# Loading one batch's v straight into rows, spreading another's in four 32-row tiles, and moving a mixer step between two transposes

## The chip, the cores and the metric

The kernel runs on one core of one Trainium2 chip. The metric is the device time of one execution in microseconds (us).

PE is the TensorE matmul stream, PEld its weight loads, DVE the vector engine, ACT the scalar engine, POOL GpSimd, SP the sync engine. "L640" is a line of the kernel's source. The same line has other numbers in the changed kernel: the mixer's hidden matmuls are L630 before and L629 after, the output matmuls L640 and L639, the spreading of v L561 and L560. In experiments that put removed code back they are L633, L643 and L564.

## The reference

Eight batches, eight heads, 576 rows, head size 64. Attention with a causal mask and a bias from a cumulative sum of s; its output is the input of a low-rank token mixer and a two-layer channel mixer.

```python
scores = q @ k.T / sqrt(64)
cum    = cumsum(max(s, 0))
scores = where(causal, -1e9, scores + min(-(cum_i - cum_j), 0))
attn   = softmax(scores);  x = attn @ v              # 8 x 576 x (8*64)
u      = x + (x.T @ U @ V).T                         # rank 32
out    = u + relu(u @ w_ch1) @ w_ch2                 # 512 -> 2048 -> 512
```

## The kernel before

Heads are worked in pairs, four pairs a batch: pair n = 4 is the first pair of batch 1. For each pair the program emits `transposes(n)` (q and k turned on PE, copied out of PSUM into a slot by ACT or DVE), `scores(n)` (matmuls, exponentials on ACT) and `values(n)` (the product with v). These are interleaved by hand with the channel mixer of an earlier batch, `chanmix`, that comes in pieces of four 512-column matmuls: `step_fill` and `fill_with` take the next pieces.

For `values`, v must lie with one row per partition (`v_slots`). Batches 2 to 7 are loaded straight into that layout, with 256-byte runs. Batches 0 and 1 were loaded raw, four rows to a partition in 1 KB runs, and PE spread them with selection matmuls:

```python
def v_tiles(b, js, copies):
    vt = v_slots[b % 3]
    if b == 0:
        pvs = [pwork() for _ in js]                  # one PSUM bank each, of four
    else:
        both = pscore()
        pvs = [both[:, ds(i * 512, 512)] for i in range(len(js))]
    for t in range(4):
        for j, pv in zip(js, pvs):
            pick, src = sel[ds(32 * j, 32), ...], v_raw[ds(32 * j, 32)]   # 32 rows of PE
            nc.tensor.matmul(pv, lhsT=pick, rhs=src[:, :, t, :], start=(t == 0), stop=...)
    for j, pv, copy in zip(js, pvs, copies):
        copy(vt[:n_rows, j, :, 0:D], pv)             # PSUM -> SBUF, DVE (batch 0), ACT (batch 1)
# ...
v_tiles(0, (0, 1), (dve, dve)); step(S2); step(S2)   # batch 0, in two pairs and a rest
v_tiles(0, (2, 3), (dve, dve)); step(S2, S2)
# ...
weave("S5 S5 T6 S5 T6 S5 S6 R0 T7 S6 R1 T7 S6 R2 S6")   # R0 to R2 spread batch 1
```

Two more pieces matter. `copies(n, hh, par)` decides which engine copies the transposes of head hh out of PSUM; for n = 4 it was ACT for head 0 and DVE for head 1. In the main loop, the token mixer of the batch before (`seqmix`) has a first step whose small result, uxT, DVE must copy before PE can go on:

```python
if n > 2 * PB and n + 1 < NP:
    run(transposes(n + 1))      # four DVE copies of the slot
step(mixing)                    # 20 small matmuls, then uxT on DVE
```

In the first 20 us PE also runs `spin` in places: matmuls on a constant whose result nobody uses, to keep PE busy over waits.

The softmax here doesn't subtract the row's maximum and nothing guards it: scores larger than these inputs give would overflow.

## Time and profile before

Time: 381.25 us median of 3 runs (381.01 to 381.28). The profile is of a further execution at full clock, which took 381.74 us, half a microsecond more than the median.

| | before |
|---|---|
| PE busy | 371.0 us of a 380.0 us span |
| matmuls | 3583 |
| ACT busy, 42 to 46 us | 4.00 of 4.00 us |
| idle PE named by its list of waits | 5.8 us, of which 1.3 before the first matmul; nearly all before 120 us |

From the page (part 1: busy time, share of the span, instructions):

```profile
PE 371.0 (98%) x3583; PEld 210.5 (55%) x3583; DVE 217.3 (57%) x453; ACT 199.8 (53%) x300; POOL 65.0 (17%) x103
```

PE's busy time says which engine to look at, not how well it does. The Trainium skill, "Trainium Kernel Development and Optimization", Performance Expectations, calls matmul busy time a bad metric, because matmuls are pipelined. So I read what PE waited for. From the list of PE's waits (us in total, times, longest; its first line, the 1.3 us before the first matmul, and the waits under 0.4 us are left out):

```profile
PE pscore L375 <- DMA slot<-hT: 1.2, 1, 1.2
PE pwork L477 <- DVE uxT L473: 0.9, 1, 0.9
PE pwork L630 <- ACT slot L310: 0.6, 1, 0.6
PE pscore L561 <- ACT v_slot L570: 0.4, 1, 0.4
```

In order: the first scores waited for the rows of s; the token mixer for uxT; a hidden matmul for a PSUM bank that ACT was still copying out; the spreading of batch 1 for ACT's copies.

The timeline of PE has start, duration, line, operands, count, and in brackets the idle time before. A group's own duration contains the pipeline's tail, so the cost of a group is the start of the next minus its own. Batch 1's spreading, and its surroundings:

```profile
50.94 0.61 PE L375 MATMUL pscore<-slot 68*128 68x128 bf16 x6
51.48 1.04 PE L561 MATMUL pscore<-hT,sel 32*128 32x512 bf16 x8
52.45 1.04 PE L640 MATMUL pwork<-w_sb,hT 128*128 128x512 bf16 x4
...
56.50 0.60 PE L375 MATMUL pscore<-slot 68*128 68x320 bf16 x4
57.47 0.59 PE L561 MATMUL pscore<-hT,sel 32*128 32x512 bf16 x2 [0.37 <-ACT v_slot L570]
57.99 1.04 PE L640 MATMUL pwork<-w_sb,hT 128*128 128x512 bf16 x4
```

Eight matmuls in two row tiles take 52.45 - 51.48 = 0.97 us; four rounds of a 512-column matmul (0.216 us each in this trace) would be 0.86. The group left out, at 54.12 us, takes 0.97 as well.

### The profile page before, as it was taken

The numbers are of one execution on the slowest core, as the hardware profiler recorded it, in microseconds if no ns is written. First come the engines' busy times: TensorE is split into PE (matmuls) and PEld (weight loads), VectorE is DVE, ScalarE is ACT, GpSimd is POOL, SyncE is SP. The second block draws the span as 40 slices with busy tenths as digits, with TensorE's granted clock in tenths as the row PEclk, the third lists the DMA queues.
The fourth block names the chain that finished last, engine by engine and source line by source line (L and its number), as shares of the span: only waits on it lengthen the run. The fifth ranks groups of instructions, "written<-read, shape, count | busy, mean of one in ns | idle before, by whom it ended". The sixth has DMA issues, their size and how long they took to land.

```text
span 380.0 us, 8508 instructions
## 1 busy us (share of the span) xinstructions
PE 371.0 (98%) x3583; PEld 210.5 (55%) x3583; DVE 217.3 (57%) x453; ACT 199.8 (53%) x300; POOL 65.0 (17%) x103
## 2 busy tenths in 40 slices
PE   8899999999999999999999999999999999999996
PEld 3575556766655666565655665666555544444443
DVE  8785356877777766876678666876753232002012
ACT  3876996657741676147724773457561530620620
POOL 8985316006001400140014000000000000000000
PEclk9999999999999999999999999999999999999999
DMA  7999999949946991599159924220313031301002
GB/s 107 174 209 205 200 160 117 151 113 121 117 41 113 161 124 21 124 160 123 23 91 169 139 32 75 75 73 19 74 47 100 19 72 68 83 28 73 11 29 83
DMA packets 86110, 37.29 MB, mean 98 GB/s; under 512 B 66424, under 2 KB 80472, under 8 KB 86072
## 3 DMA queue, kind: packets, MB, share of 16 engines
q0 software_dynamic: 47216, 18.44, 49.3%
q1 hardware_dynamic: 38856, 18.31, 25.8%
q8 instruction: 28, 0.46, 0.5%
q14 instruction: 10, 0.08, 0.1%
HBM read 37.25 MB, written 9.70 MB: 124 GB/s over the span
## 4 chain that ended last, share of the span: by engine, by line
PE 88%; ACT 6%; DVE 3%; DMA 2%; issue 1%; SPq 0%; ACTq 0%; DVEq 0%
PE pwork L640 31%; PE pwork L630 30%; PE pscore L375 10%; PE pwork L435 8%; PE pwork L293 3%; ACT pT L390 1%; ACT slot L310 1%; ACT hT L662 1%; DMA slot<-hT 1%; PE pwork L677 1%; PE pscore L630 1%; PE pwork L464 1%; DVE uT L489 1%; DVE slot L310 1%; DMA hT<-in_s_dram 1%
## 5 line engine op out<-in xcount | busy, mean ns | idle before, releaser
L630 PE MATMUL pwork<-uT,w_sb 128*128 128x512 bf16 x560 | 135.1, 379 | 1.0 <-ACT slot L310 0.6
L640 PE MATMUL pwork<-w_sb,hT 128*128 128x512 bf16 x560 | 135.3, 379 | 0.2 <-ACT hT L662 0.2
L662 ACT ACTIVATE hT<-pwork 128x512 bf16<-128x512 f32 x140 | 84.4, 608 | 86.9 <-PE pwork L630 86.6
L310 DVE COPY slot<-pwork 64x576 bf16<-64x576 bf16 x111 | 88.8, 800 | 12.3 <-PE pwork L293 10.0
L390 ACT ACTIVATE pT<-pscore 128x1024 bf16<-128x1024 f32 x57 | 57.4, 1025 | 59.8 <-PE pscore L375 59.8
L630 PEld LDWEIGHTS <-w_sb 128*128 128x128 bf16 x576 | 51.0, 98 | 51.7 <-issue 2.3
L640 PEld LDWEIGHTS <-hT 128*128 128x128 bf16 x560 | 49.0, 98 | 50.2 <-issue 2.9
L700 DVE TENSOR_TENSOR o_sb<-pwork,u_sd 128x512 f32<-128x512 f32 x31 | 21.4, 691 | 65.1 <-PE pwork L640 64.4
L375 PE MATMUL pscore<-slot 68*128 68x128 bf16 (+1 forms) x506 | 54.9, 246 | 1.3 <-DMA slot<-hT 1.2
L375 PEld LDWEIGHTS <-slot 68*128 68x128 bf16 x570 | 41.8, 97 | 23.9 <-issue 1.5
L320 DVE TENSOR_TENSOR pT<-pT,keep 128x512 bf16<-128x512 bf16 (+1 forms) x81 | 28.6, 353 | 38.4 <-ACT pT L407 23.2
L435 PEld LDWEIGHTS <-pT 128*128 128x128 bf16 x870 | 32.4, 97 | 10.1 <-issue 0.3
L435 PE MATMUL pwork<-v_slot,pT 128*128 128x65 bf16 x870 | 34.5, 194 | 0.0
L445 DVE TENSOR_TENSOR x_sb<-pwork,rec 128x320 bf16<-128x320 f32 x64 | 31.4, 491 | 2.1
L401 ACT ACTIVATE pT<-pscore 128x1024 bf16<-128x1024 f32 x29 | 30.2, 1040 | 2.9 <-PE pwork L375 1.5
L108 POOL DMA_DIRECT2D q_sd<-in_q_dram x12 | 9.4, 782 | 122.1 <-PE pwork L293 114.5
L225 POOL DMA_DIRECT2D v_slot<-in_v_dram x24 | 21.3, 902 | 10.5 <-DMA w_sb<-in_moe_w_ch_dram 8.2
L444 DVE RECIPROCAL rec<-pwork 128x5 f32<-128x5 f32 x64 | 12.2, 191 | 16.3 <-PE pwork L435 15.7
L293 PEld LDWEIGHTS <-q_sd 72*128 72x128 bf16 x256 | 14.7, 98 | 10.0 <-DMA q_sd<-in_q_dram 0.9
L293 PE MATMUL pwork<-identity,q_sd 72*128 72x72 bf16 x256 | 18.0, 196 | 0.0
L293 PE MATMUL pwork<-identity,k_sd 72*128 72x72 bf16 x256 | 17.9, 198 | 0.1
L310 ACT COPY slot<-pwork 64x576 bf16<-64x576 bf16 x17 | 13.5, 797 | 1.4 <-PE pwork L293 1.2
(110 smaller groups left out, 202.5 us busy)
## 6 DMA issues: line engine op xcount, KB each, us to landing
out_dram<-o_sb SPq DMA_DIRECT2D x35, 256.0 KB
w_sb<-in_moe_w_ch_dram POOLq DMA_DIRECT2D x4, 1024.0 KB, 12.0
q_sd<-in_q_dram POOLq DMA_DIRECT2D x6, 576.0 KB, 8.7
k_sd<-in_k_dram POOLq DMA_DIRECT2D x6, 576.0 KB, 13.8
v_slot<-in_v_dram POOLq DMA_DIRECT2D x24, 128.0 KB, 15.6
hT<-in_v_dram POOLq DMA_DIRECT2D x2, 512.0 KB, 13.6
q_sd<-in_q_dram POOLq DMA_DIRECT2D x4, 144.0 KB, 5.0
k_sd<-in_k_dram POOLq DMA_DIRECT2D x4, 144.0 KB, 5.8
```

What stands on the lines that cost most here:

```text
L293: nc.tensor.transpose(tps[hh][:, c, t2, :], src[:, 2 * hp + hh, ds(t2 * 128, 128)], identity[:TP, :TP],)
L310: copies(n, hh, par)(dst[:, :, :, :, par], tp[par * D : par * D + D].rearrange("p c t m -> p c m t"),)
L320: nc.vector.tensor_tensor(dst, dst, keep[:, :, 0:w].to_broadcast([128, n_tiles, w]), op=ALU.min)
L375: nc.tensor.matmul(dst, lhsT=slot[0:KA, hh, ds(S + j * 128, 128)], rhs=slot[0:KA, hh, lo:hi], start=True, stop=True,)
L390: nc.scalar.activation(pT[:, hh, 0:1024], near, EXP, scale=scale)
L401: nc.scalar.activation(pT[:, :, 1024:1536], mid.rearrange("p (a b) -> p a b", a=2), EXP, scale=scale)
L435: nc.tensor.matmul(po[:, i, :], lhsT=pT[:, hh, ds(place(j, i), 128)], rhs=vt[:, j, h, :], start=(j == 0), stop=(j == i), skip_group_check= ...
L445: nc.vector.tensor_tensor(x_sb[:, hp, :, ds(hh * D, D)], po[:, :, 0:D], rec.to_broadcast([128, 5, D]), op=ALU.mult,)
L630: nc.tensor.matmul(f1, lhsT=w1_sb[:, kt, ds(nf * 128, 128)], rhs=u[:, kt, :], start=(kt == 0), stop=(kt == 3),)
L640: nc.tensor.matmul(f2, lhsT=hT[:, nf, ds(i * 128, 128)], rhs=w2_sb[:, nf, :], start=(nf == 0), stop=(nf == NF - 1 and not more), skip_grou ...
L662: nc.scalar.activation(hT[:, nf, :], f1, RELU)
L700: nc.vector.tensor_tensor(o_sb.rearrange("p (a b) -> p a b", a=4), f2.rearrange("p (a b) -> p a b", a=4), u_sd[:, :, i, :], op=ALU.add,)
```

## The change

The intent: take PE work and PE idle time out of the first 120 us.

1. v of batch 1 is loaded like that of batches 2 to 7; its 18 spreading matmuls and five ACT copies go, and one piece of the channel mixer is put in at two places (word "F").
2. v of batch 0 is spread in four 32-row tiles at once. The group stands behind two steps of scores (six matmuls each) and two `spin` matmuls.
3. The rows of s for head 1 of pair 0 are sent before those of head 0.
4. For pair 4, DVE copies head 0 and ACT head 1.
5. The token mixer's first step stands between the two heads' transposes; the order at the very end is changed a little.

```diff
-        for hh in range(2):
+        for hh in (1, 0) if n == 0 else (0, 1):
             nc.sync.dma_start(out=slots[n][D:KA, hh, 0 : 2 * S], ...)
...
-        on_act = hh == 0 and (n in (0, 1, 4, 5, 7, 8, 9, 10) or n == 2 and par == 0)
+        on_act = hh == (n == 4) and (n in (0, 1, 4, 5, 7, 8, 9, 10) or n == 2 and par == 0)
...
-        if b == 0:
-            pvs = [pwork() for _ in js]
-        else:
-            both = pscore()
-            pvs = [both[:, ds(i * 512, 512)] for i in range(len(js))]
+        pvs = [pwork() for _ in js]
+        if len(js) == 4:
+            spin(2, pvs[0])
+            yield
...
-    v_tiles(0, (0, 1), (dve, dve))
     step(S2)
+    vs = v_tiles(0, (0, 1, 2, 3), (dve, dve, dve, dve))
+    step(vs)
     step(S2)
-    v_tiles(0, (2, 3), (dve, dve))
+    drain(vs)
     step(S2, S2)
...
-    load_v_raw(1)
-    init_v(nc.gpsimd, v_slots[1])
+    load_v(1)
...
-    weave("S5 S5 T6 S5 T6 S5 S6 R0 T7 S6 R1 T7 S6 R2 S6")
-    weave("V4 V4 S7 V5 S7 V5 S7 T8 S7 T8 V6 V6 S8 V7 S8 V7 T9 S8 T9")
-    weave("S8 S9 M1 S9 M1 M1 S9 M1 S9 M1 M1")
+    weave("S5 S5 T6 S5 T6 S5 S6 T7 S6 T7 S6 F S6")
+    weave("V4 F V4 S7 V5 S7 V5 S7 T8 S7 F T8 V6 V6 S8 V7 S8 V7 T9 S8 T9")
+    weave("S8 S9 M1 S9 M1 S9 M1 M1 S9 M1 M1")
...
         if b == B:
             fill_with(3)
-            step(mixing)
-            fill_with(2)
-            step(mixing)
-            fill_with(2)
+            for _ in range(3):
+                step(mixing)
+                fill_with(2)
         if n > 2 * PB and n + 1 < NP:
-            run(transposes(n + 1))
-        step(mixing)
+            for at, _ in enumerate(transposes(n + 1)):
+                step_fill()
+                if at == 0:
+                    step(mixing)
```

More of the change, by code (lines that the diff above doesn't have):

```diff
@@ L794 @@
     nc.gpsimd.memset(pT_early[1][:, :, 1600:], 1.0)
-    v_tiles(0, (4,), (dve,))
+    drain(v_tiles(0, (4,), (dve,)))
     step(S3)
@@ L847, in weave @@
         for word in order.split():
+            if word == "F":
+                fill_with(1)
+                continue
             kind, n = word[0], int(word[1:])
@@ L853, in weave @@
                     made[word] = scores(n, pT_of(n))
-                elif kind == "R":
-                    v_tiles(1, ((0, 1), (2, 3), (4,))[n], (act, act))
-                    made[word] = iter(())
                 elif kind == "V":
```

## The prediction

> **What bounds it now.** TensorE: by the page 371.0 us busy of a 380.0 us span, and 88% of the chain of waits. The stretches view shows full granted clock, and almost no idle PE from 130 us to the last matmul. So only PE work or PE idle time removed counts. The list of PE's waits holds about 5 us, nearly all before 120 us: first rows of s (slot from hT) 1.17 us at 12.96; bank held by ACT's slot copy 0.64 us at 37.00; v copies on ACT 0.37 us at 57.47; uxT copy on DVE 0.90 us at 113.00.
>
> **Terms of the change, in us of PE's chain (timeline of PE).**
>
> 1. Batch 1's spreading matmuls (18 of 32 rows x 512) go away. In the timeline they cost with their lead-in 1.07 (at 51.4), 1.07 (at 54.0), and at 57.5 0.52 plus 0.53 idle. Sum 3.2. Five ACT copies of 0.59 go too. The added fill steps only move work. Saving 3.2.
>
> 2. Batch 0's spreading: 16 matmuls in two pairs cost 2 x 0.97. As four tiles at once I estimate one group of 0.97, from the seqmix step, whose four 32-row x 512 matmuls take 0.33 us together although one alone takes 0.216. The Trainium skill, "TensorEngine Tiling (Array Packing)", Key Properties, says that tiles run in parallel and that changing the mode drains the engine; this trace agrees (0.33 for four, about 0.10 lead at a switch). Two spins give back 0.43. But all four banks become ready together and later than the first pair does now, and DVE then needs 5 copies of 0.65 to 0.68 in a row; tile 4's copy would end near 23.1 us instead of 22.8, and values(0) waits for it. Together with term 3, I credit only 0.3 at the end of values(0).
>
> 3. Rows of head 1 issued first: the issues on SP are 0.57 us apart, so head 1's scores and the ACT chain start that much earlier. Mostly absorbed by term 2's copies.
>
> 4. Pair 4's copies swapped between ACT and DVE: ACT comes to its copies only at 35.35, after two ReLUs; DVE should free the first bank about 0.7 earlier. Saving 0.5 of the 0.64.
>
> 5. Mixer's first step between the transposes: the uxT copy no longer queues behind four slot copies on DVE (0.80 each). Saving 0.9 at 113; nothing later, where PE doesn't wait.
>
> **Risk.** v of batch 1 becomes 4608 short packets instead of 1280. Short ones pass at about 700 per us (2172 in the 3 us from 54 us): 6.5 us instead of 3.5, from k's landing at 46.1 on, so landed near 52.6 to 54. values(4) starts at 58.9 now and would at about 55. It should just hold. GpSimd's issues already wait for older transfers (3.6 and 4.65 us), so the last part may be issued only at 44 to 46. Landing late stalls PE 1 to 3 us.
>
> **Sum.** 3.2 + 0.3 + 0.5 + 0.9 = 4.9, less 0.2 for new small waits: 381.2 - 4.7 = 376.5 us, 1.2% faster. Range 374.3 to 378.6. Chances: faster by over 2% 0.06, within 2% 0.92, slower 0.02.
>
> **What will show it.** No batch-1 spreading group; batch 0's sixteen matmuls within about 1 us; no PE wait for uxT near 110 and none over 0.2 at the pair-4 transposes; values(0) ending 0.2 to 0.5 earlier; values(4) not waiting for v's DMA.
>
> **What would make it wrong.** v landing after 55 us; the 16 matmuls not overlapping four ways (loss 0.9); freed PE time turning into waits on ACT, which is 96% busy from 40 to 50 us.

## More of the kernel before

All comparisons are between runs in the fast state, at the full granted clock unless the text says otherwise. A TensorE clock below full speed is reported for each run as its mean over the span.

## The result, and the profile after

377.26 us median of 4 runs (376.57 to 378.68), against 381.26 us of the kernel before (381.01 to 381.44, 4 runs). The ratio is 0.990, 95% interval 0.987 to 0.993. Ratios here are the mean time of one kernel's fast runs over that of the other's fast runs of the same rounds, so they are not quite the ratio of the medians. The time is inside the predicted range, 0.8 us above the predicted 376.5.

The runs of the changed kernel lie 2.1 us apart; those of before lie 0.4 us apart. The profile that came with the result is of the slowest of them, 378.68 us. Its page and its list of PE's waits:

```profile
PE 367.9 (98%) x3567; PEld 211.2 (56%) x3567; DVE 217.3 (58%) x453; ACT 197.0 (52%) x295; POOL 67.9 (18%) x106
```

```profile
PE pwork L293 <- DMA k_sd<-in_k_dram: 1.3, 2, 0.7
...
PE pwork L629 <- DVE o_sb L715: 0.5, 1, 0.5
PE pwork L629 <- ACT hT L661: 0.4, 1, 0.4
PE pwork L560 <- DVE v_slot L569: 0.4, 1, 0.4
PE pwork L293 <- DMA q_sd<-in_q_dram: 0.4, 1, 0.4
PE pwork L435 <- DVE uT L489: 0.4, 1, 0.4
PE pwork L435 <- DMA v_slot<-in_v_dram: 0.3, 1, 0.3
```

In this run all four waits shown of before are gone (in the control run below the first scores do wait for the rows of s again, 0.7 us). In their place are others, and the largest is for DMA: k of pairs 6 and 8. The last part of batch 1's v is late by 0.3 us too. At the place where batch 1 was spread, the timeline of PE now reads:

```profile
51.08 0.61 PE L375 MATMUL pscore<-slot 68*128 68x128 bf16 x6
51.52 0.30 PE L293 MATMUL pwork<-identity,q_sd 72*128 72x72 bf16 x4
...
55.58 0.59 PE L435 MATMUL pwork<-v_slot,pT 128*128 128x65 bf16 x14
56.49 0.20 PE L435 MATMUL pwork<-v_slot,pT 128*128 128x65 bf16 x1 [0.32 <-DMA v_slot<-in_v_dram]
```

Batch 0's sixteen matmuls in four tiles:

```profile
18.90 1.13 PE L560 MATMUL pwork<-hT,sel 32*128 32x512 bf16 x16
19.96 0.61 PE L375 MATMUL pscore<-slot 68*128 68x320 bf16 x4
...
21.32 0.59 PE L560 MATMUL pwork<-hT,sel 32*128 32x512 bf16 x2 [0.38 <-DVE v_slot L569]
```

Sixteen take 19.96 - 18.90 = 1.06 us here (0.98 in the control run below), little more than the eight of before, so the four tiles do run at once.

**An account by stages.** A single total can't separate five parts of half a microsecond each. PE's program is fixed, and where no DMA comes late, most of its stages repeat to 0.02 us from run to run. So I cut the timeline of PE at the starts of matmul groups that every kernel has, and compare before with the changed kernel's control run (`after_again` below, 377.27 us, close to the median). The run of before that has the profile is a slow one of its kind, 381.74 us, so the sum below is 4.4 us where the totals differ by 4.0. Differences of start times in us:

| stage | before | changed | difference |
|---|---|---|---|
| start to values(0) | 22.98 | 23.04 | +0.06 |
| to the transposes of pair 4 | 10.96 | 11.07 | +0.11 |
| to the first output matmul | 16.14 | 16.03 | -0.11 |
| to values(4) | 8.84 | 5.37 | -3.47 |
| to the last output group | 314.58 | 313.55 | -1.03 |
| sum | 373.50 | 369.06 | -4.44 |

Nearly all of the gain lies in one stage, that of batch 1's spreading. In the first 50 us nothing was gained between these two profiles, though three of the five parts aim there. In the slow profile above (378.68), the third stage is 0.5 us longer than in the control and the last 1.3 us, where the DMA waits are.

### The profile page after: what moved, and what is told of

The parts are those of the page before. It is cut to its first block, busy times and chain, and to the rows that moved or that the text cites. A ratio compares the mean times of both kernels' runs of the same rounds, so it can differ in the third digit from the quotient of the medians.

```text
span 377.0 us, 8475 instructions
## 1 busy us (share of the span) xinstructions
PE 367.9 (98%) x3567; PEld 211.2 (56%) x3567; DVE 217.3 (58%) x453; ACT 197.0 (52%) x295; POOL 67.9 (18%) x106
## 4 chain that ended last, share of the span: by engine, by line
PE 79%; DMA 11%; ACT 4%; issue 2%; DVE 2%; POOL 1%; DVEq 0%; ACTq 0%; POOLq 0%
PE pwork L639 29%; PE pwork L629 28%; PE pscore L375 8%; PE pwork L435 7%; DMA w_sb<-in_moe_w_ch_dram 5%; DMA k_sd<-in_k_dram 4%; PE pwork L293 3%; DMA q_sd<-in_q_dram 2%; ACT pT L390 1%; PE pwork L676 1%; PE pwork L464 1%; DVE uT L489 1%; ACT pT L401 1%; ACT hT L661 1%; PE pwork L560 0%
## 5 line engine op out<-in xcount | busy, mean ns | idle before, releaser
L375 PE MATMUL pscore<-slot 68*128 68x128 bf16 (+1 forms) x506 | 55.8, 246 | 0.1
L225 POOL DMA_DIRECT2D v_slot<-in_v_dram x28 | 24.9, 904 | 11.3 <-DMA k_sd<-in_k_dram 3.6
```

The lines of the kernel that those rows point to most:

```text
L225: nc.gpsimd.dma_start(out=vt[:, t, :, 0:D], in_=v[b, :, ds(t * 128, 128), :].rearrange("h p d -> p h d"),)
L375: nc.tensor.matmul(dst, lhsT=slot[0:KA, hh, ds(S + j * 128, 128)], rhs=slot[0:KA, hh, lo:hi], start=True, stop=True,)
```

## The experiments

My first theory after the result: the straight load saved about 3.5 us of PE and gave some 1.8 back in DMA waits; the swap for pair 4 and the four tiles are worth nothing; the mixer step is worth about 1 us. The rivals: the loss is elsewhere, or the waits are chance. First each part was undone by itself.

### undo_v1: batch 1 raw and spread on PE again

```diff
-    load_v(1)
+    load_v_raw(1); init_v(nc.gpsimd, v_slots[1])
-    weave("... T7 S6 T7 S6 F S6") ; weave("V4 F V4 ... S7 F T8 ...")
+    weave("... R0 T7 S6 R1 T7 S6 R2 S6") ; weave("V4 V4 ... S7 T8 ...")
```

> The changed kernel with batch 1's v loaded raw and spread on TensorE again (fill words as before). Theory: taking the spreading away saved about 3.5 us of PE and gave back about 1.8 in new waits for DMA (k of pair 6, v of batch 1, k of pair 8), so this should run 1.4 to 2.2 us slower than the changed kernel, near 379.2, with no DMA wait of PE after 20 us and a spread between runs under 0.6 us. Rival A: the spreading part is worth its full 3.2 and something else gave time back: near 380.5. Rival B: DMA waits and spread stay here: then they don't come from v's load.

Measured: 380.96 us median of 6 (380.02 to 381.52), ratio to before 0.9981 (0.9968 to 0.9993). The control has 0.9892, so the part is worth 0.0089 x 381.5 = 3.4 us (0.9 either way, by the two intervals). My theory expected 1.4 to 2.2 and falls; rival A holds. Against before, the same run says what the other four parts give together: 0.0019 x 381.5 = 0.7 us (0.3 to 1.2). The stage to values(4) is 8.84 us, exactly that of before. The PE waits for DMA of the slow profile aren't there, but they aren't in the control either. The spread isn't under 0.6 us. Its slowest run has a mean clock of 0.996.

### undo_v0: batch 0 in pairs again

```diff
-    step(S2); vs = v_tiles(0, (0, 1, 2, 3), ...); step(vs); step(S2); drain(vs)
+    drain(v_tiles(0, (0, 1), ...)); step(S2); step(S2); drain(v_tiles(0, (2, 3), ...))
```

> The changed kernel with batch 0's spreading in pairs again. Theory: four at once is worth nothing, because DVE starts its five copies later (values(0) then starts 5.6 us after the last scores of pair 1, 5.25 before): 376.8 to 377.4, the same as the changed kernel or 0.2 to 0.4 better. Rival: it saves the half microsecond of PE that it removes: 377.8.

Measured: the two fast runs are 377.23 and 377.56 us (0.9893), the same as the changed kernel, as the theory said. The other two are 387.79 us at a mean clock of 0.969 and 383.13 at 0.987. The profile is of the first of these. Its stretches (start and end, length, then PE, PEld, DVE, ACT, POOL busy; then PE's granted clock, the DMA share and GB/s):

```profile
5.00:10.00 5.00, 4.24 (x55) 2.67 (x56) 4.54 (x7) 2.98 (x4) 4.93 (x9) 1.00 1.01 135
10.00:15.00 5.00, 3.47 (x31) 2.18 (x33) 1.59 (x2) 2.11 (x4) 4.90 (x10) 0.62 1.05 143
15.00:20.00 5.00, 4.86 (x37) 3.28 (x37) 4.00 (x5) 3.19 (x5) 3.29 (x9) 0.50 1.21 185
...
30.00:35.00 5.00, 5.00 (x49) 3.50 (x48) 2.12 (x6) 2.97 (x4) 1.77 (x4) 0.50 0.75 142
35.00:40.00 5.00, 4.92 (x119) 4.50 (x118) 4.14 (x15) 2.06 (x4) 3.48 (x5) 0.99 0.22 19
```

PE waited 1.31 us for q of pair 2, up to 11.68 us; the granted clock went to 0.50 and came back only after 35 us. The Trainium skill, "TensorE: Matmul & The Clock Gate", Part 1, describes a gate that halves PE's clock after idleness. The 0.50 agrees; the page's idle window of about 3.4 us doesn't, for the longest wait before the fall was 1.31 us. That the wait brought the clock down is argued from the order in time, not tested. It is no property of this kernel alone: the kernel before had such a run, 391.94 us at 0.969, one of 11.

### undo_swap: pair 4's copies on the old engines

```diff
-        on_act = hh == (n == 4) and (...)
+        on_act = hh == 0 and (...)
```

> The changed kernel with pair 4's copies on the old engines. Theory: the swap takes away the 0.64 us wait at 37 us, but ACT stays saturated until 46 us and the time comes back at 40.8 and 41.4 us: 377.3, a difference under 0.2. Rival (as predicted): 0.5 slower, 377.8. Expect the 0.64 wait back in the list of PE's waits, and the waits of 0.2 and 0.4 gone.

Measured: 376.95 us (376.60 to 377.31, 4 runs), 0.9881 (0.9868 to 0.9894): no loss. The stages show why. From the transposes of pair 4 to its scores the old form takes 3.93 us and the new one 3.11; from there to the run of 24 hidden matmuls the old takes 3.87 and the new 4.58. Of 0.82 us won, 0.71 are given back; 0.11 stay. The wait that went, before:

```profile
34.46 1.90 PE L630 MATMUL pwork<-uT,w_sb 128*128 128x512 bf16 x8
37.00 1.02 PE L630 MATMUL pwork<-uT,w_sb 128*128 128x512 bf16 x4 [0.64 <-ACT slot L310]
```

In the control these twelve matmuls run without a wait, and the two waits at which the time is given back are:

```profile
40.36 0.60 PE L375 MATMUL pscore<-slot 68*128 68x320 bf16 x4
41.17 0.22 PE L375 MATMUL pwork<-slot 68*128 68x64 bf16 x2 [0.21 <-ACT slot L310]
41.80 5.34 PE L629 MATMUL pwork<-uT,w_sb 128*128 128x512 bf16 x24 [0.40 <-ACT hT L661]
```

### undo_mix: the token mixer's first step after both transposes

```diff
-            for at, _ in enumerate(transposes(n + 1)):
-                step_fill()
-                if at == 0:
-                    step(mixing)
+            run(transposes(n + 1))
+        step(mixing)
```

The order at the end was to be put back too; by my mistake one `fill_with(3)` more than before stands there. The stage after 115 us is 254.95 us in this run and 254.94 in the control, but that hides two differences which cancel (below), and the mistake may have a part in one.

> The changed kernel with the mixer's first step after both transposes again, and the old order at the end. Theory: 0.9 to 1.1 slower (378.3), all of it at 110 us, where PE waits for uxT again. Rival: worth nothing, as other work would fill it: 377.3.

Measured: 377.48 us (377.24 to 377.57, 4 runs), 0.9894 (0.9881 to 0.9907). Against the control's 0.9892 the total doesn't show the 0.9 to 1.1 us that I expected, and it can't settle it: the interval is half a microsecond to each side, and runs of different chips are compared. The trace tells more. The wait is back:

```profile
108.72 0.61 PE L375 MATMUL pscore<-slot 68*128 68x128 bf16 x6
109.95 0.23 PE L477 MATMUL pwork<-identity,uxT 128*128 128x128 bf16 x1 [0.62 <-DVE uxT L473]
```

From the first hidden matmul of the next channel mixer to the end of this token mixer, this run takes 35.94 us and the control 35.15, where the same matmul doesn't wait:

```profile
109.67 0.22 PE L477 MATMUL pwork<-identity,uxT 128*128 128x128 bf16 x1
```

So the part is worth 0.79 us at this point. It doesn't simply stay so. Compared at the last matmuls of each token mixer, this run is 0.28 us behind the control at 114 us (before the wait it was 0.51 ahead), still 0.29 at 190 us, but only 0.02 at 267 us; at the last output group it is 0.29 behind again. It makes up about 0.26 us on the way and loses as much again at the end, where the order was changed too. There PE's next group starts 0.37 us after the start of the last token mixer's last group in this run and before, and 0.11 in the control. `v0_alone` below has the same code at the end as this run, and 0.11, so that gap isn't explained by the end's order alone. The 0.79 us is thus what part 5 as a whole is worth, my mistake included; the moved step alone is worth between 0.5 and 0.8.

### after_again: the changed kernel, as control

> The changed kernel unaltered, as the control on the chip of this call. Its first profile (378.68 us, its slowest run) had PE waits for DMA of 1.3 us (k), 0.4 (q) and 0.3 (v). If those are chance, a run near 377 shows less than 0.5 us of them; if they come with the change in every run, a run near 377 shows them too.

Measured: 377.27 us median of 5 (376.49 to 378.82), 0.9892 (0.9873 to 0.9911). The profile is of the run of 377.27. After 20 us it has no DMA wait over 0.2 us at all. So the waits for k and v of the first profile are chance, and don't come in every run. Of the nine runs of the changed kernel two are over 378.6 us: the first profile's, with 1.6 us of waits for k and v, and one here at a mean clock of 0.995.

### raw_idle: the old packets, the new PE program

```diff
-    load_v(1)
+    load_v_raw(1); nc.gpsimd.memset(v_slots[1], 0.0); init_v(nc.gpsimd, v_slots[1])
```

Nobody spreads what is loaded, so the result is wrong.

> The changed kernel, but batch 1's v comes by the old raw load of 1280 long packets and nobody spreads it: its slot is only cleared (wrong result on purpose). PE's work is that of the changed kernel, the packets are those of before. Theory: the 4608 short packets delay k of pairs 6 and 8 and v itself, so without them the DMA waits and the spread go: 0.3 to 0.8 us faster than the control. Rival: the packets cost nothing that PE sees: same as the control within 0.2.

Measured: 377.42 us (377.04 to 378.32, 4 runs), 0.9896 (0.9882 to 0.9910). Same as the control; the rival holds. In a usual run the 4608 short packets cost nothing that PE sees. In one profile it has a wait of its own, 0.92 us in values(7) at 67.6 us, that the trace doesn't name. So this run doesn't tell whether the short packets make late landings more frequent.

### w2_late: the second half of w_ch2 after v of batch 1

```diff
-    load_w2(0); load_w2(1); load_qk(1, 4, 4); ...; load_v(1)
+    load_w2(0); load_qk(1, 4, 4); ...; load_v(1); load_w2(1)
```

> The changed kernel with the second half of w_ch2 loaded after q, k and v of batch 1 instead of before them. Theory: q and k of pair 6 and v of batch 1 land some 5 us earlier, so no wait for them; 0.2 to 0.5 faster than the control and a smaller spread. Risk: that half lands after 56 us and a chanmix output waits for it. Rival: same within 0.2.

Measured: 376.60 us (376.39 to 377.25, 4 runs), 0.9874 (0.9860 to 0.9887). The mean is better than the control's, but the intervals overlap, and its stages after values(0) are the control's to 0.02 us, except one that is 0.11 shorter. Inconclusive by itself; see `best` for what it does together with `act_relief`.

### undo_rows: the rows of s in the old order

```diff
-        for hh in (1, 0) if n == 0 else (0, 1):
+        for hh in range(2):
```

> The changed kernel with the rows of s for pair 0 sent in the old order. Theory: the first scores start 0.6 us later, and PE gives back nearly all of it before values(0), since DVE and ACT set the pace there: 0.1 to 0.3 slower than the control. Rival: the full 0.57 is lost.

Measured: 377.08 us (376.53 to 377.37, 4 runs), 0.9879 (0.9864 to 0.9894); the total shows no loss. In the traces, the first scores of pair 0 start at 12.96, 12.84 and 12.63 us in the three kernels with the old order (before, this, `v0_alone`), on average 12.81. In the ten profiles with the new order at full clock there, they start between 11.50 and 12.69, on average 12.15. So the order is worth about 0.66 us at that point, but the landing of the first DMAs moves it by more than that from run to run, and with three profiles of the old order this is a hint.

### v0_alone: the kernel before with only the four tiles

The changes 1, 3, 4 and 5 are all undone (with the same extra `fill_with(3)` at the end).

> The kernel before with only batch 0's spreading as four tiles at once (and its two spins). Theory: in the timeline of PE, from the first scores of pair 0 to values(0) takes 10.4 us as in every kernel with the change, against 10.02 before: the four-tile form costs 0.4 us although it takes away 0.9 us of matmuls, because all five DVE copies start after its end. Time 381.4 to 382.0, no gain. Rival (the form is worth its matmuls): under 9.7 us there, 380.9.

Measured: 381.65 us (380.94 to 381.86, 4 runs), ratio 1.0002 (0.9986 to 1.0018): no gain. From the first scores to values(0) it takes 10.41 us; the kernel before takes 10.02. So much of the theory holds, and not by one profile only: with pairs it is 10.02 and 10.04 (before, `best`), with the four tiles 10.40 to 10.92 in ten profiles at full clock. The reason is only in part the expected one. Before, the first pair's spreading and DVE's copies, in two lots:

```profile
17.89 1.04 PE L561 MATMUL pwork<-hT,sel 32*128 32x512 bf16 x8
18.96 1.29 DVE L570 CAST v_slot<-pwork 128x512 bf16<-128x512 f32 x2 [0.52 <-PE pwork L561]
20.92 1.88 DVE L570 CAST v_slot<-pwork 128x512 bf16<-128x512 f32 x3 [0.67 <-PE pwork L561]
```

In this run, in one (the changed kernel's first profile has it 0.31 us earlier, with the last copy's end at 23.05):

```profile
19.21 1.04 PE L564 MATMUL pwork<-hT,sel 32*128 32x512 bf16 x16
20.28 3.07 DVE L573 CAST v_slot<-pwork 128x512 bf16<-128x512 f32 x5 [1.60 <-PE pwork L564]
```

In both forms the first copy starts 1.07 us after the first spreading matmul: sixteen matmuls take no longer than eight, so handing four banks over together delays no copy. And the five copies then run without a gap, 3.07 us from first to last where before it was 3.84. But the spreading itself starts 6.58 us after the first scores instead of 4.93, because it stands behind two steps of scores and two spins, and so the last copy ends at 23.35 us instead of 22.80. Values(0) doesn't wait for that copy itself; PE waits earlier, 0.23 and 0.38 us, for a bank that the copies must free (the second is the wait of the batch's last two matmuls, shown at 21.32 us above for the first profile). What is shown is that this form in this place costs 0.4 us. Four tiles without the spins, or in the place of the first pair, weren't run, so that four tiles as such are worth nothing isn't shown.

### act_relief: ACT freed of pair 5's copies

```diff
-  (n in (0, 1, 4, 5, 7, 8, 9, 10)
+  (n in (0, 1, 4, 7, 8, 9, 10)
```

> The changed kernel with all of pair 5's copies on DVE, so that ACT loses 1.6 us near 39 us. Theory: swapping pair 4's copies made the stretch from the transposes of pair 4 to its scores 0.8 us shorter and the next, to the run of 24 hidden matmuls, 0.7 us longer, because ACT has no slack there. With ACT relieved the second stretch falls from 4.57 to about 3.9 us and 0.5 to 0.7 us reach the end. Rival (the second stretch is held by DVE or by banks): it stays at 4.57 or grows.

Measured: 376.43 us (376.36 to 377.57, 4 runs), 0.9875 (0.9856 to 0.9894). The stretch falls from 4.58 to 3.84 us, and both waits are gone:

```profile
39.86 0.60 PE L375 MATMUL pscore<-slot 68*128 68x320 bf16 x4
40.30 0.22 PE L375 MATMUL pwork<-slot 68*128 68x64 bf16 x2
40.56 5.59 PE L629 MATMUL pwork<-uT,w_sb 128*128 128x512 bf16 x24
```

So ACT had held it. But the run of 24 then takes 0.25 us more, and the stage after it 0.22 (0.17 of which is a wait for q of pair 6): from the scores of pair 4 to the first output matmul, 12.65 us against 12.92. Of 0.74 us, 0.27 get through, less than the 0.5 to 0.7 I expected.

### best, best_again: w2_late, pairs for batch 0, and act_relief together

> The changed kernel, plus the second half of w_ch2 after v of batch 1, plus batch 0's spreading in pairs, plus all of pair 5's copies on DVE. If the parts add: 0.4 from the head, 0.5 to 0.7 from ACT, fewer late DMA waits, so 375.6 to 376.2. If the two spins were needed to keep the clock up, some runs fall into a lower clock after 12 us and lose 5 to 10 us.

> The same kernel as best, more rounds, because its gain over the changed kernel is under one per cent. If the gain is real its fast runs stay near 0.986 of the kernel before (the changed kernel: 0.989 and 0.990) and under 376.6 us. If it was chance, 0.989 and 377.2. A run at a lower clock would show that the spins dropped from it had a use.

Measured: 376.14 us (375.76 to 376.50, 4 runs), 0.9862 (0.9844 to 0.9880); then, on another chip, 376.53 us (376.04 to 380.25, 6 runs), 0.9871 (0.9854 to 0.9887). Eight of the ten runs are at most 376.55 us, about 0.9 us better than the changed kernel's median. The profile of the fast run of 375.97 shows where: from the first scores to values(0) 10.04 us against 10.41, and from the scores of pair 4 to the first output matmul 12.44 against 12.92. The second is more than `act_relief` alone gave (12.65): with `w2_late` added its wait of 0.17 us for q of pair 6 is gone, and here 0.48 of the 0.74 us get through. The other two runs, 379.17 and 380.25, have a mean clock of 0.991. The profile of the first shows what went before the fall:

```profile
17.43 1.04 PE L560 MATMUL pwork<-hT,sel 32*128 32x512 bf16 x8 [0.61 <-DMA hT<-in_v_dram]
18.40 1.06 PE L375 MATMUL pscore<-slot 68*128 68x128 bf16 x12
19.39 1.33 PE L560 MATMUL pwork<-hT,sel 32*128 32x512 bf16 x8
```

```profile
16.00:20.00 4.00, 3.39 (x34) 1.86 (x34) 3.67 (x5) 2.87 (x5) 3.94 (x11) 1.00 1.26 231
20.00:24.00 4.00, 4.00 (x23) 1.95 (x20) 1.98 (x3) 2.42 (x5) 3.34 (x6) 0.50 1.16 204
24.00:28.00 4.00, 4.00 (x74) 3.54 (x72) 1.77 (x6) 2.64 (x4) 1.27 (x2) 0.65 1.16 208
```

PE now came to the spreading at 17.4 us, before batch 0's raw v had landed. It waited, and the clock was halved soon after. In the changed kernel the spreading starts later, behind two steps of scores and two spins (18.90 us), and none of its profiles has a wait for the raw v. So the form of part 2 costs 0.4 us in a good run and seems to buy safety. Counting all runs: with the pairs and the new order of rows, 4 of 14 had a mean clock under 0.992; with the four tiles, none of 43 had less than 0.995; of the kernel before, with the pairs and the old order, 1 of 38. That is a hint and not a proof: in `undo_v0` the fall came at 12 us, before this code, and `undo_v1`, which has the four tiles, was at half clock for some 3 us in its slowest run too. I don't claim a version that beats the changed kernel safely. The combination of w2_late and act_relief with the four tiles kept would be the next to try; it wasn't run.

## Why the prediction was right

The time, 377.26 us, lies in the range 374.3 to 378.6, and within 2% was given 0.92. The terms, as predicted and as the stages or undone parts show them (us):

| term | predicted | measured |
|---|---|---|
| 1. batch 1's spreading | 3.2 | 3.47 (stage), 3.4 (undo_v1) |
| 2 and 3. four tiles and order of rows | 0.3 | 0.66 - 0.39 = 0.27 |
| 4. swap for pair 4 | 0.5 | 0.11 |
| 5. mixer step (with the end's order) | 0.9 | 0.79 |
| sum (predicted: less 0.2 for new waits) | 4.9 | 4.6 |

The measured terms come from single traces, and their sum is above what the totals give: 381.26 - 377.26 = 4.0 us, and by the ratio 2.7 to 5.0. Terms 2 to 5 add up to 1.2 here; `undo_v1` has 0.7 (0.3 to 1.2) for them. Part of the hit is that errors cancel: the first term came larger than predicted and the fourth smaller.

1. Right, and for the reason given. Its size was a sum of starts read off PE's timeline, and it includes the 0.53 us in which PE stood idle before the third group. It left out another gap of 0.27 us, before the scores at 56.50 us, and that is the difference to the measured 3.47.

2 and 3. Right in size, and in part in mechanism. The matmuls overlap four ways (0.98 to 1.06 us for sixteen), and DVE's five copies set the pace. The sum can be read at the predicted point as well: values(0) started at 22.98 us before, and in the eight full-clock profiles with both parts at 22.42 to 23.10, on average 22.71, which is 0.27 earlier. The copy's end was predicted at 23.1 us and came at 23.05 in the first profile, but at 23.36 in the control. That "values(0) waits for it" was not seen: its first thirty matmuls take 0.92 us in both kernels, in the changed one they start before that copy has ended, and PE's waits for DVE come earlier, for banks. And the copies start late because of the place of the group, spins included, more than because "all four banks become ready together".

4. The mechanism was right, the size wrong. The step that failed is "Saving 0.5 of the 0.64": the wait at 37 us went, 0.8 us was won there, and 0.7 was lost again four microseconds later. The prediction had named the danger itself, "freed PE time turning into waits on ACT, which is 96% busy from 40 to 50 us", but didn't put it into this term. `act_relief` shows that it was ACT.

5. Right at 113 us: the wait is gone, and this is worth 0.79 us there. "Nothing later" is not shown: in `undo_mix` 0.26 us comes back by 267 us and goes again at the end, and the trace doesn't say why.

The risk: "It should just hold" is right for usual runs (the control had no wait for v) and not for all. In the slowest run of the first call the last part of v came 0.3 us late. The prediction did not see that k of pairs 6 and 8 could come late as well: these waits were 1.3 us in that run. GpSimd issued the five parts of v between 30.2 and 40.2 us, earlier than the 44 to 46 that I had feared for the last.

My theory after the result did worse than the prediction: it took the waits of one profile, of the slowest of four runs, for a standing cost. The control and `undo_v1` refuted it. What makes some runs 1.5 us slower isn't settled: in one it was late k and v, in others the clock. Of the stage to the end, 1.03 us, part 5 as a whole explains 0.79; I have not assigned the other 0.24, which lie among many small changes in order.

## What to carry to other kernels

Work that a DMA can do in its access pattern is worth taking off the bottleneck engine, and its worth can be read off the timeline beforehand as the start of the next group minus the start of this one. Making a step faster on one engine gains nothing if it must also start later, or if the next engine is saturated: follow the gain for some microseconds before you book it. When several parts are each under the noise of the total, cut the trace at points that all versions share; here most stages repeat to 0.02 us while totals spread over 2 us. Two stages can also differ and cancel, so compare at several points and not only at the end. And profile a typical run, of both kernels, before you explain a loss or a gain.

## What the Trainium skill lacked or had wrong

- "TensorE: Matmul & The Clock Gate", Part 1, says that about 3.4 us of sustained activity bring the full clock back (its own caveats leave room for longer spells). In `undo_v1` half clock did last for only some 3 us. But in `undo_v0` it stayed at 0.50 for 20 us (15 to 35 us) with PE busy 4.86 to 5.00 us of every 5; in `best_again` it was 0.50 from 20 to 24 us and 0.65 on average from 24 to 28, with PE busy throughout. That fall followed a wait of 0.61 us in a stretch that had PE busy 3.39 of 4.00 us; the page doesn't say how much scattered idleness is enough.
- "TensorEngine Tiling (Array Packing)", Key Properties, says that changing the tiling mode drains the engine, without a size. Here a group of eight 32-row matmuls in two tiles took 0.97 us and one of sixteen in four tiles 0.98 to 1.06, for 0.86 us of streaming: 0.1 to 0.2 us a visit, which is then the most that the change of mode can have cost here.
- The same page's PSUM Bottleneck section warns that evacuation may become the limit, and gives no size for it. Here five copies of up to 128x512 took 3.07 us on DVE in a row, after 0.98 us of matmuls in four tiles, and PE waited 0.23 and 0.38 us for a bank.
